# A memory-attention and feed-forward kernel: one quarter of the first 384 tokens in float16 halves, and a new order of all steps

## The chip, the cores and the metric

The kernel runs on one core of a Trainium2 chip. The metric is the time of one execution in microseconds (us); the table below gives the median of three runs. A profiled execution has a time of its own and a span, from its first instruction to its last. The engines are TensorE (PE, matrix products; its weight loads are shown as PEld), VectorE (DVE), ScalarE (ACT) and GpSimd (POOL); SyncE (SP) issues the transfers (DMA). Products are written to PSUM; all other tiles lie in SBUF.

## What is computed

The input has 8 batches of 8 heads, 576 positions and a head size of 64, with 32 memory slots per head. The feed-forward network has 512 inputs and 2048 hidden units.

```python
def _attn_ref(q, k, v, phi):
    a = softmax(phi)                        # over the 32 slots
    k_m = einsum('bhsm,bhsd->bhmd', a, k)
    v_m = einsum('bhsm,bhsd->bhmd', a, v)
    attn = softmax(q @ k_m.T / sqrt(64))    # over the 32 slots
    return attn @ v_m

def _moe_ref(x, w_in, w_out):
    h = x @ w_in
    g = maximum(0.01 * h, h)
    return g @ w_out
...
x = attn_out.transpose(0, 2, 1, 3).reshape(4608, 512)
return _moe_ref(x, w_in, w_out)
```

`softmax` is shorthand for the reference's maximum, exponential, sum and quotient. Both weight matrices come as 64-bit floats, 8 MB each.

## The kernel before

The kernel never forms the attention's output. For each batch it multiplies the memory values by `w_in` beforehand ("fold"), so that the first product of the network takes the attention weights `a` (8 heads by 32 slots, 256 rows) instead of the 512 features. The 2048 hidden units are cut into four quarters of 512, and these into 16 blocks of 128.

Tokens go through the network in groups. Groups 0, 1 and 2 are 384 tokens each, from batches 0 and 1; the later groups take 256 tokens, from batches 2 to 7. For each group and each pair of blocks ("unit" u, 8 of them) there is an up step (`up_products`, into `ph`), an activation (`leaky`) and a down step (`down_products`, three tiles of 128 tokens by 512 outputs, summed over all units in three PSUM tiles `po`).

Group 0 is done in float32: two matmuls of 128x384 per up step, with the folded weights in `w32`, and three of 128x512 per down step, against the float32 matrix in `wo`. All other groups are done in float16 halves: each operand is a high and a low part, and three products (high by high, low by high, high by low) stand for one, so 6 matmuls per up step and 9 per down step. A scalar factor per quarter scales the parts.

The weights are read as 64-bit words and made into float32 by integer and activation steps (`load`, `low`, `high`, `put`), their squares are summed for a bound (`squares`, lines 409 to 411), and later they are split into halves (`hi_part`, `lo_part`).

Every step has a name, and two long strings, `OPENING` and `LATER`, give the order in which the steps are issued; each engine runs its own instructions in that order. The names that matter below:

- `a0.phi`, `a0.k`, `a0.v`, `a0.q`: loads of batch 0. `A1`: the maximum of phi on VectorE (line 592), `A2`, `A3`, `B0`: the maximum spread over partitions (TensorE, lines 633 and 649, with VectorE between), `B1`, `B2`: subtraction and exponential (lines 658 and 664), `B3`: sums (lines 680 to 683), `C1`: products with k and v (line 698; `C10` is k, `C11` is v in batch 0), `C2`: the transposed sums (line 712), `C3`: scaled copies, `D1`: transposes (lines 777 and 785), `D3`, `D5`: copies (`D5` makes `vT`, line 805), `Q`: transposes of q (line 845), `E1`: scores (line 887; `E10` is its first half), `E2`: transposes of the scores (line 908), `S`: softmax of the scores, whose sixth step writes the weights `a`.
- `i0.ld1`, `i0.h1`, `i0.y1`, `i0.t1`, `i0.b`: load, low, high, put of piece 1, and squares, of quarter 0 of `w_in`; `o` stands for `w_out`. A piece is 768 or 512 columns. The loads go through eight buffers in turn.
- `f00.1`, `f00.2`: the fold of quarter 0 for batch 0 (line 1020) and its two copies to `w32` (line 1378). `W03.p`, `W03.h0`, `W03.l0`: the fold of batch 0, quarter 3 into halves.
- `u6.P0`, `u6.V0`, `u6.O0`: up step, activation and down step of group 0 (lines 1114, 1121, 1191); `P8`, `V8`, `C8`, `L8`, `O8` the same for groups 1 and 2, with the split into halves on VectorE (`C`, `L`). `p`, `v`, `s`, `c`, `l`, `d`, `x`, `z`: the later groups. `Z`: a tile's copy out and store.
- `z.4`: four float32 matmuls of ones, 128x512, that compute nothing ("idle products", line 1395). There are nine of them in four steps.
- `end0`, `end1`: the two halves of the last tile's output, copied by ScalarE and VectorE (lines 1176 and 1178), each with two stores issued by ScalarE and two by SyncE.

Of the kernel before, what the change touches and what calls it, by code (L numbers as in the profile page):

```python
# [22 lines left out]
A_SCALE = 2.0**13  # L23
# [27 lines left out]
i2.b u4.V0 a1.B20 u5.P0 a1.B3 o0.b a1.C10 i3.ld2 a1.Q0 i3.ld1 a1.C2 u5.V0 o1.b u2.O1 i3.y0 u5.P1
u4.V1 a1.C30 a1.C31 a1.C3k a1.C4 a1.D10 a1.D2 o2.b i3.h0 a1.D3 a1.Q1 i3.y2 i3.h2 a1.D11 a1.D4 u3.O1
i3.t2 a1.E1 o3.ld0 a1.D5 i3.y1 u4.O0 i3.h1 i3.t0 o3.h0 u5.V1 o3.y0 o3.ld2 u5.O0 a1.E20 i3.t1 a1.E21
i3.b ci.1 o3.ld1 a1.E22 f03.1 a1.S01 a1.S11 a1.S02 a1.S03 a1.S04 u4.O1 o3.y2 o3.y1 o3.h2 ci.2 o3.t0
f03.2 a1.S12 ci.3 ci.4 e. o3.h1 o3.t1 a1.S05 u6.P0 u6.V0 a1.S13 a1.S06 a1.S07 u6.P1 u7.P0 a1.S14
a1.S15 o3.t2 w0.2 u7.V0 u6.O0 a1.S16 o3.b w1.1 co.1 co.2 u7.O0 w1.2 co.3 u6.V1 co.4 u5.O1 o0.k0
a1.S08 o0.k1 o0.k2 u7.P1 e2. o0.l0 u7.V1 o0.l1 u6.O1 a1.S17 a1.S18 o0.l2 u7.O1
# [10 lines left out]
W01.h1 a2.phi a2.kv2 a2.kv1 o0.s0 W01.h0 a2.A1 Z0.0 o0.s1 a2.kv0 W01.l0 o0.m0 W01.l1 o0.m1 o0.n0  # L68
o0.n1 Z0.1 o0.s2 i0.k1 Z0.2 P8.0 P8.1 W11.p V8.0 a2.kv3 P9.0 o0.s3 V8.1 W11.h1 C8 P9.1 L8 W11.h0
a2.A2 W11.l1 V9.0 o1.k0 a2.A4 W11.l0 V9.1 O8.0 W02.h0 o1.l0 W02.h1 C9 o1.k1 O8.1 W02.l1 o1.k2 W02.l0  # L70
o0.m2 L9 o0.m3 W12.p o1.l2 o1.l1 P10.0 W12.h0 o0.n2 P10.1 V10.0 i0.k0 W12.l0 W12.h1 P11.0 o1.s0
V10.1 i0.k2 W12.l1 O9.0 V11.0 C10 o1.m0 o0.n3 L10 P11.1 o1.s1 O9.1 W03.h1 o1.n0 W03.h0 o3.s3 V11.1
P12.0 o1.m1 O10.0 C11 V12.0 o1.n1 L11 P12.1 o1.s2 O10.1 o1.m2 W03.l1 o1.s3 V12.1 W03.l0 a2.A3 o1.n2
o2.k0 C12 W13.p o2.k2 o2.l0 W13.h1 P13.0 W13.h0 W13.l1 P13.1 W13.l0 V13.0 o2.k1 L12 V13.1 O11.0
# [1419 lines left out]
```

## Time and profile before

| | |
|---|---|
| median of three runs | 648.58 us (647.6 to 649.02) |
| the profiled execution's own time | 647.19 us |
| its span | 645.3 us |
| TensorE busy | 632.7 us |
| VectorE, ScalarE, GpSimd busy | 515.0, 391.2, 29.5 us |
| moved by DMA | 61.16 MB |

The profiled execution took 647.19 us, 1.9 us more than its span; the runs that were timed are others. In the lines below, a row of the timeline gives start, duration, engine, source line, operation, output and inputs, sizes, the number of instructions merged into the row, and in brackets the idle time ahead of it with what ended it. The trace records a float32 matmul as two instructions. A row of the table by stretches gives the stretch and its length, busy time and instructions of PE, PEld, DVE, ACT and POOL, then TensorE's granted clock, the DMA engines' share, and GB/s.

### The profile page before, as it was taken

What the parts mean: (1) busy time and instruction counts of PE and PEld (TensorE: products, weight loads), DVE (VectorE), ACT (ScalarE), POOL (GpSimd) and SP (SyncE); (2) the same over time, 40 slices, a digit from 0 to 9 for tenths busy, and PEclk for the clock granted to TensorE, in tenths of its full rate; (3) what the DMA queues carried; (4) which work ended last, traced back from release to release, by engine and by line L of the source; (5) the groups of instructions that cost most, each with busy time, mean ns of one, the idle gap of its engine ahead of it and who ended that gap; (6) DMA issues with size and microseconds to landing.
All of it is one profiled execution on the core that took longest, in us unless ns stands there. A gap on an engine that the chain in (4) does not pass through costs nothing.

```text
span 645.3 us, 17189 instructions
## 1 busy us (share of the span) xinstructions
PE 632.7 (98%) x7304; PEld 480.4 (74%) x7304; DVE 515.0 (80%) x863; ACT 391.2 (61%) x671; POOL 29.5 (5%) x37
## 2 busy tenths in 40 slices
PE   6799999999999999999999999999999999999997
PEld 3445445665545788888888888897888888889896
DVE  5875889998997899899969975789977897575641
ACT  2898868765563556467556665655675476564543
POOL 0010111000001001002000010000010001000000
PEclk9999999999999999999999999999999999999999
DMA  9999813005601644431253011064104110010102
GB/s 263 405 389 290 279 44 118 15 13 99 196 3 31 139 156 66 124 105 42 33 138 124 6 30 42 22 125 149 34 20 85 18 30 23 13 28 8 34 1 51
DMA packets 85501, 61.16 MB, mean 95 GB/s; under 512 B 62000, under 2 KB 68656, under 8 KB 85424
## 3 DMA queue, kind: packets, MB, share of 16 engines
q1 hardware_dynamic: 85232, 59.94, 33.2%
q8 instruction: 57, 0.93, 0.6%
q14 instruction: 20, 0.16, 0.1%
q10 hardware_dynamic: 192, 0.13, 0.1%
HBM read 50.59 MB, written 9.45 MB: 93 GB/s over the span
## 4 chain that ended last, share of the span: by engine, by line
PE 94%; DMA 3%; ACT 1%; DVE 1%; issue 0%; SPq 0%; ACTq 0%
PE po L1302 31%; PE ph L1234 22%; PE po L1191 16%; PE ph L1114 8%; PE ph L1302 5%; PE pa L1020 4%; PE pa L698 3%; DMA arena<-in_moe_w_in_dram 2%; PE po L1339 2%; PE pa L861 1%; DMA wo<-in_k_dram 1%; DMA arena<-in_q_dram 0%; ACT arena L397 0%; ACT wi L411 0%; PE pa L887 0%
## 5 line engine op out<-in xcount | busy, mean ns | idle before, releaser
L1302 PEld LDWEIGHTS <-arena 128*128 128x128 f16 x2184 | 209.8, 98 | 31.9 <-issue 8.6
L1250 ACT ACTIVATE wi<-ph,g_sc 128x256 f32<-128x256 f32 (+1 forms) x224 | 98.6, 465 | 160.9 <-PE ph L1234 155.8
L1234 PE MATMUL ph<-a,w_mem 128*128 128x256 f16 (+3 forms) x1440 | 144.8, 246 | 0.1
L1234 PEld LDWEIGHTS <-w_mem 128*128 128x128 f16 x1440 | 114.5, 98 | 13.8 <-issue 3.0
L1302 PE MATMUL po<-wo,arena 128*128 128x256 f16 x936 | 122.1, 273 | 0.0
L1302 PE MATMUL po<-arena 128*128 128x256 f16 x936 | 122.0, 273 | 0.0
L1191 PE MATMUL po<-wo,arena 128*128 128x512 f16 (+1 forms) x384 | 110.3, 433 | 0.0
L1279 DVE TENSOR_TENSOR arena<-arena 128x1024 f16<-128x1024 f32 x52 | 63.5, 1221 | 21.9 <-ACT arena L1275 21.9
L1279 DVE TENSOR_TENSOR arena<-wi,arena 128x768 f16<-128x768 f32 (+1 forms) x60 | 54.7, 911 | 9.5 <-ACT arena L1275 9.5
L1271 DVE TENSOR_TENSOR arena<-wi 128x256 f32<-128x256 f32 x104 | 40.4, 430 | 25.4 <-ACT wi L1250 24.8
L1275 ACT CAST arena<-arena 128x1024 f16<-128x1024 f32 x52 | 54.4, 1046 | 7.9 <-DVE arena L1271 7.6
L1114 PE MATMUL ph<-a,w_mem 128*128 128x192 f16 (+2 forms) x304 | 52.2, 317 | 0.0
L1191 PEld LDWEIGHTS <-arena 128*128 128x128 f16 x288 | 27.9, 98 | 29.6 <-issue 0.6
L1275 ACT CAST arena<-wi 128x768 f16<-128x768 f32 (+1 forms) x60 | 46.6, 776 | 1.5
L1271 DVE TENSOR_TENSOR arena<-wi,arena 128x256 f32<-128x256 f32 x104 | 45.7, 439 | 1.8
L1302 PE MATMUL ph<-wo,arena 128*128 128x256 f16 x312 | 42.6, 273 | 0.0
L985 POOL TENSOR_TENSOR a<-t,a 128x1024 f16<-128x1024 f32 (+2 forms) x16 | 21.9, 1384 | 428.1 <-ACT a L980 428.1
L1191 PEld LDWEIGHTS po<-wo,arena 128*128 128x128 f32 x96 | 17.7, 190 | 20.3 <-issue 18.2
L1020 PE MATMUL pa<-wi,vT 64*32 64x512 f16 (+1 forms) x704 | 28.9, 420 | 1.2 <-ACT vT L805 1.2
L1114 PEld LDWEIGHTS <-w_mem 128*128 128x128 f16 x240 | 20.7, 98 | 10.3 <-issue 4.1
L1121 ACT ACTIVATE arena<-ph,g_sc 128x384 f32<-128x384 f32 x32 | 18.4, 581 | 15.7 <-PE ph L1114 15.4
L1053 ACT ACTIVATE w_mem<-pa 128x512 f16<-128x512 f32 x40 | 22.7, 596 | 7.5 <-PE pa L1020 6.6
(216 smaller groups left out, 752.9 us busy)
## 6 DMA issues: line engine op xcount, KB each, us to landing
out_dram<-obs SPq DMA_DIRECT2D x140, 64.0 KB, 1.7
arena<-in_k_dram SPq DMA_DIRECT2D x28, 288.0 KB, 4.6
arena<-in_v_dram SPq DMA_DIRECT2D x28, 288.0 KB, 5.1
arena<-in_q_dram SPq DMA_DIRECT2D x96, 72.0 KB, 2.8
arena<-in_moe_w_in_dram SPq DMA_DIRECT2D x12, 512.0 KB, 9.6
arena<-in_moe_w_out_dram SPq DMA_DIRECT2D x8, 768.0 KB, 7.9
arena<-in_phi_dram SPq DMA_DIRECT2D x7, 576.0 KB, 5.6
arena<-in_q_dram SPq DMA_DIRECT2D x4, 576.0 KB, 8.7
```

Of the source, the lines that this page charges most:

```text
L698: nc.tensor.matmul(var["pk"][g][hh * M:(hh + 1) * M, cs], ld["phi"][rows, hh, j, :], ld["kv", hh][rows, kinds[0]:kinds[-1] + 1, j, :], sta ...
L985: nc.gpsimd.tensor_tensor(piece(lo, tb), piece(t2, tb), piece(hi, tb), ALU.subtract)
L1020: nc.tensor.matmul(pf[g][cols, :], lhs, rhs, start=(n == 0), stop=(n == len(passes) - 1), tile_position=(g * D, hh * M),)
L1053: nc.scalar.activation(tiles(halves(w16(b, j), g)[:, 0]), w(g), AF.Copy, scale=ws)
L1114: nc.tensor.matmul(ph[:, t0:t0 + n * SB], lhs, rhs, start=(m == 0), stop=(m == len(seq) - 1))
L1191: nc.tensor.matmul(po, lhs, rhs, start=(f == 0 and m == 0), stop=(f == NQ * NF - 1 and m == len(seq) - 1),)
L1234: nc.tensor.matmul(ph[:, t0:t0 + n], lhs, rhs, start=(m == 0), stop=(m == len(seq) - 1))
L1250: nc.scalar.activation(dst, ph, AF.Prelu, scale=g_sc2[:, j:j + 1], alpha=SLOPE)
L1271: nc.vector.tensor_tensor(gt[:, x], y, z, op)
L1275: nc.scalar.copy(dst[:, 0], src)
L1279: nc.vector.tensor_tensor(dst[:, 1], src, dst[:, 0], ALU.subtract)
L1302: nc.tensor.matmul(acc, g[:, x, s, u], rhs, start=(h == 0 and j == 0 and u == 0 and m == 0), stop=(j == NQ - 1 and u == 1 and m == 2), ski ...
```

## The change

Quarter 3 of group 0 (units 6 and 7) leaves the float32 path. Its up steps take halves of the folded weights and halves of `a`, which two new steps make (`A0.h`, `A0.l`); its activation goes through the split that groups 1 and 2 use (`u6.C`, `u6.L`). The sums over quarters 0 to 2 lie in three PSUM tiles under another scale, so they are copied aside first (`Y0`, ScalarE), their places are used anew for quarter 3, and at the end one VectorE instruction for each tile scales that result and adds what was set aside. The fold of quarter 3 for batch 0 goes straight from PSUM into halves; the step `f03` is gone. Groups 1 and 2 run through the quarters in the order 3, 2, 1, 0.

```diff
+    Q32 = NQ - 1
...
     wi_s, wo_s = (
-        [t.bitcast(F16).rearrange("p (i x) -> p i x", i=2) for t in ts[:NQ]] for ts in (wi, wo)
+        [t.bitcast(F16).rearrange("p (i x) -> p i x", i=2) for t in ts]
+        for ts in (wi[:NQ], wo[2:] + wo[:1])
...
+    def full(G, u):
+        return G == 0 and u < 2 * Q32
...
+    def quarter(G, u):
+        return u // 2 if G == 0 else NQ - 1 - u // 2
...
+    def a0_part(i):
+        src = a_f32(0)[:, 0:2].rearrange("p tb (g x) -> p tb g x", g=NG)
+        hi, lo = a0_halves[:, :, 0], a0_halves[:, :, 1]
+        if i == 0:
+            nc.scalar.copy(hi, src)
+        else:
+            nc.gpsimd.tensor_tensor(lo, src, hi, ALU.subtract)
...
-            if G == 0:
+            if full(G, u):
                 seq = [
-                    (w32[f // NF][g][:, fs], a_f32(b)[:, tb:tb + n, g * SB:(g + 1) * SB])
+                    (w32[j][g][:, fs], a_f32(b)[:, tb:tb + n, g * SB:(g + 1) * SB])
                     for g in range(NG)
                 ]
             else:
                 seq = [
-                    (halves(w16(b, f // NF), g)[:, x, fs], a[:, tb:tb + n, y, g, :])
+                    (halves(w16(b, j), g)[:, x, fs], a[:, tb:tb + n, y, g, :])
                     for g in range(NG) for x, y in ((0, 0), (1, 0), (0, 1))
                 ]
...
+    def set_aside(t):
+        nc.scalar.activation(obs[:, t * E:(t + 1) * E], pos["32"][t], AF.Copy, scale=1.0 / WT)
...
     def store(G, t, po):
         ob = obs[:, t * E:(t + 1) * E]
-        nc.scalar.activation(ob, po, AF.Copy, scale=row_scale(G, t))
+        if G == 0:
+            nc.vector.scalar_tensor_tensor(ob, po, row_scale(G, t), ob, ALU.mult, ALU.add)
+        else:
+            nc.scalar.activation(ob, po, AF.Copy, scale=row_scale(G, t))
         send(G, t, ob)
...
-        if G == 0:
+        if full(G, u):
             seq = [(g[:, i, cs], wo[j + 1][:, es])]
         else:
             seq = [(g[:, x, i, cs], wo_s[j][:, y, es]) for x, y in ((0, 0), (0, 1), (1, 0))]
...
-a0.phi0 a0.A10 z.4 a0.phi1 a0.A11 a0.A2 a0.k a0.A3 a0.B0 a0.q0 a0.B10 a0.B11 a0.B20 a0.q1 a0.B21
+a0.phi0 a0.phi1 a0.A11 a0.A10 a0.A2 a0.A3 a0.B0 a0.B10 a0.B20 a0.k a0.B11 a0.B21 a0.C10 a0.B3 a0.C2
...
-z15.0 d53.2 p55.3 v55.3 c55.1 z15.1 d53.3 l55.1 d54.0 d54.1 d54.2 d54.3 d55.0 d55.1 end0 d55.2 d55.3
-end1
+d53.3 d54.0 d54.1 d54.2 d54.3 d55.2 d55.0 d55.3 d55.1 end1 end0
```

The buffers of the split halves move with the order of the quarters (the halves of `w_out` into `wo2`, `wo3`, `wo4`, `wo0`; the sums of pairs of blocks that the later groups use start in `wo1`). Both strings of steps are new throughout. Three places of the new order follow.

TensorE at the very start of the program, before (L1395 are the idle products, L633 and L649 are A2 and B0, L698 is C10):

```order
L1489 UNCONDITIONAL_BRANCH
L1395 MATMUL pa<-ones 128x512 x4
L633 MATMUL pa<-ident,r1k 128x128
L649 MATMUL pa<-r1k,ones 64x128 x2
L698 MATMUL po<-wo_92,wi_88 32x64 x2
```

and in the changed program, whose lines for the same steps are 635, 651 and 700:

```order
L1520 UNCONDITIONAL_BRANCH
L635 MATMUL pa<-ident,r1k 128x128
L651 MATMUL pa<-r1k,ones 64x128 x2
L700 MATMUL po<-wo_92,wi_88 32x64 x2
L700 MATMUL po<-wo_93,wi_88 32x64 x2
```

The four idle products at the head are gone from there; A2 is TensorE's first work.

TensorE from C2 (L712) over D10 (L777) and the two halves of the scores (L887) to the products with v (L698), before:

```order
L712 MATMUL po<-ident,r1k 128x128
L1395 MATMUL pa<-ones 128x512
L777 MATMUL pa<-ident,x_k 96x128 x4
L887 MATMUL pa<-wi_87,kT 32x192 x24
L887 MATMUL pa<-wo_91,kT 32x192 x24
L1395 MATMUL pa<-ones 128x512 x3
L698 MATMUL po<-wo_92,wi_88 32x64 x2
```

and in the changed program:

```order
L714 MATMUL po<-ident,r1k 128x128
L1431 MATMUL pa<-ones 128x512 x3
L779 MATMUL pa<-ident,x_k 96x128 x4
L1431 MATMUL pa<-ones 128x512
L889 MATMUL pa<-wi_87,kT 32x192 x24
L889 MATMUL pa<-wo_91,kT 32x192 x24
L1431 MATMUL pa<-ones 128x512 x4
L700 MATMUL po<-wo_92,wi_88 32x64 x2
```

Three idle products stand ahead of D10 where one stood, one more ahead of the scores, and four behind them where three stood.

ScalarE at the end of the program, before (L1250 are activations, L1275 casts, L1326 scales a finished tile, L1176 is the copy of `end0`, L1165 issues stores):

```order
L1275 CAST arena<-wi_89 128x256
L1326 ACTIVATE obs<-obs,osc 128x512
L1176 ACTIVATE obs<-po,osc 128x256
L1165 DMA out_dram<-obs 32x256 x4
L1489 UNCONDITIONAL_BRANCH
```

and in the changed program:

```order
L1303 CAST arena<-wi_89 128x256
L1184 DMA out_dram<-obs 32x256 x2
L1201 ACTIVATE obs<-po,osc 128x256
L1184 DMA out_dram<-obs 32x256 x2
L1520 UNCONDITIONAL_BRANCH
```

The two stores of `end1`'s half now stand ahead of the copy of `end0`'s; on TensorE the last down steps are d55.2, d55.0, d55.3, d55.1 in place of d55.0 to d55.3.

More of the change, by code (lines that the diff above doesn't have):

```diff
@@ L51 @@
[L51 to L56, printed above, removed]
@@ L67 @@
 LATER = """
[L68 to L72, printed above, removed]
@@ L1049, in w @@
         def w(g):
-            return tiles(w32[j][g]) if b == 0 else by_tile(src["w"][g])
+            return tiles(w32[j][g]) if b == 0 and j < Q32 else by_tile(src["w"][g])
         def hi_part(g):
@@ L1119, in leaky @@
     def leaky(dst, ph, G, u):
-        sc = H_SCALE0 if G == 0 else g_sc[:, u // 2:u // 2 + 1]
+        sc = H_SCALE0 if full(G, u) else g_sc[:, quarter(G, u):quarter(G, u) + 1]
         nc.scalar.activation(dst, ph, AF.Prelu, scale=sc, alpha=SLOPE)
@@ L1189, in down_products @@
             seq = [(g[:, x, i, cs], wo_s[j][:, y, es]) for x, y in ((0, 0), (0, 1), (1, 0))]
+        u0, u1 = (0, 2 * Q32) if full(G, u) else (2 * Q32 if G == 0 else 0, NU)
         for m, (lhs, rhs) in enumerate(seq):
             nc.tensor.matmul(
-                po, lhs, rhs, start=(f == 0 and m == 0),
-                stop=(f == NQ * NF - 1 and m == len(seq) - 1),
+                pos["32" if full(G, u) else G][t], lhs, rhs, start=(f == 2 * u0 and m == 0),
+                stop=(f == 2 * u1 - 1 and m == len(seq) - 1),
             )
     def down(G, u, i):
-        if (u, i) == (0, 0):
-            pos[G] = [ps_o.tile([P, E], F32, name="po") for t in range(NT)]
+        if i == 0 and u in (0, 2 * Q32 if G == 0 else 0):
+            pos["32" if full(G, u) else G] = [
+                ps_o.tile([P, E], F32, name="po") for t in range(NT)
+            ]
         for t in range(NT):
@@ L1372 @@
         opening(u)
-    for j in range(NQ):
+    for i, key in enumerate("hl"):
+        steps[f"A0.{key}"] = lambda i=i: a0_part(i)
+    for t in range(NT):
+        steps[f"Y0.{t}"] = lambda t=t: set_aside(t)
+    for j in range(Q32):
         def products(j=j):
@@ L1381 @@
         bounds(kind, steps)
-    steps["e."] = fold_scales
+    for b in range(FB):
+        steps[f"e{b}."] = lambda b=b: fold_scales(b)
     for b in range(B):
@@ L1400 @@
         steps[f"z.{n}"] = lambda n=n: idle_products(n)
-    def all_bounds():
-        even_out()
-        for b in range(FB):
-            out_scale(b)
-    steps["e2."] = all_bounds
+    steps["e2."] = even_out
     def unit(m):
```

291 lines of the change are left out of this document (153 added, 138 removed).

## The prediction

> **What bounds the kernel now.** I read the page's shares first, then a table of busy time by stretch, then the list of what TensorE waited for.
>
> ```profile
> span 645.3 us, 17189 instructions
> ...
> PE 632.7 (98%) x7304; PEld 480.4 (74%) x7304; DVE 515.0 (80%) x863; ACT 391.2 (61%) x671; POOL 29.5 (5%) x37
> ...
> 20.00:30.00 10.00, 7.82 (x171) 3.75 (x172) 9.11 (x18) 8.35 (x14) 0.87 (x2) 1.00 1.03 410
> 30.00:640.00 610.00, 609.90 (x6862) 468.86 (x6861) 493.56 (x826) 375.86 (x649) 27.77 (x28) 1.00 0.31 84
> ...
> PE po L698 <- ACT wi L664: 1.7, 1, 1.7
> ```
>
> From 30 to 640 us TensorE is busy 609.90 of 610.00 us at a granted clock of 1.00, and the longest wait on the list, 1.7 us for the exponential of phi, belongs to the first 30 us, as all others do. So the time has three parts that add up: an **opening** until the first product of the feed-forward network, an unbroken **stream** of matmuls whose length is the sum of its instructions, and a **tail** of a few microseconds. An engine beside TensorE matters only where it makes the stream pause. The execution took 647.19 us, its span 645.3; the median of the three timed runs, 648.58, lies 1.39 above it. I work out a difference and add it to both.
>
> **The stream.** These pieces of the chain that ended last give the price of a matmul where matmuls of one kind follow each other.
>
> ```profile
> 31.10 2.58 PE ph L1114 x8
> 33.68 2.57 PE po L1191 x6
> ...
> 116.67 1.94 PE po L1191 x9
> ...
> 144.83 1.95 PE ph L1114 x12
> ```
>
> A float32 matmul is recorded as two. Up products in float32 (384 columns): 2.58 / 4 = 0.645 us each; down products in float32 (512 columns): 2.57 / 3 = 0.857; in float16, 1.95 / 12 = 0.1625 and 1.94 / 9 = 0.2156. The last quarter of group 0 is four blocks of 128 units. Each had 2 float32 up products and 3 float32 down products, and now has 6 and 9 in float16.
>
> - Up: 4 x (2 x 0.645 - 6 x 0.1625) = 4 x 0.315 = 1.26 us less.
> - Down: 4 x (3 x 0.857 - 9 x 0.2156) = 4 x 0.631 = 2.52 us less.
>
> The stream gets **3.8 us** shorter, all of it on the path. The fold of quarter 3 runs as the same 8 float32 matmuls as before, now as step W03.p. Reversing the quarters of groups 1 and 2, and moving the sums' buffers, changes operands and no count. What is added lies beside TensorE: three copies of 128x512 out of PSUM on ScalarE (Y0), two casts and two subtractions on VectorE, a cast of 128x768 on ScalarE and a subtraction on GpSimd (A0); two ScalarE copies of the old quarter go. Their cover is the 39% of the span in which ScalarE is idle, and u6.P0, W12.p, P9 and P8.0, which stand on TensorE between the last float32 product of the group and the first into the new accumulators. Without that cover three copies of about 0.6 us would cost 1.8.
>
> Whether the new order keeps the stream unbroken the trace cannot show. The tightest place that I find is batch 1's attention: before, two up steps and a down step stood on TensorE between B0 and C10; now only two up steps do (4 x 0.645 = 2.6 us), against a subtraction and an exponential in between.
>
> ```profile
> L658 DVE TENSOR_TENSOR arena<-arena,pa 128x1152 f32<-128x1152 f32 x1 | 1.4, 1354 | 0.9 <-PE pa L649 0.9
> L664 ACT ACTIVATE arena<-arena 128x1152 f32<-128x1152 f32 x7 | 8.1, 1157 | 0.4 <-DVE arena L658 0.4
> ```
>
> 1.35 + 1.16 plus two hand-overs is 2.6: no slack, and a pause of 0 to 0.5 us. I put pauses at 0.2 us, from 0 (as before) to 1.0 (two more such places).
>
> **The opening.** Here are TensorE's rows up to the first product, then the rows of VectorE and ScalarE that it waits for.
>
> ```profile
> 0.99 6.34 PE L1395 MATMUL pa<-ones 128*128 128x512 f32 x8 [0.99 <-POOL ones L269]
> 7.17 0.27 PE L633 MATMUL pa<-ident,r1k 128*128 128x128 f32 x1
> ...
> 10.54 0.37 PE L698 MATMUL po<-wo,wi 64*32 64x64 f32 x10 [1.68 <-ACT wi L664]
> ...
> 11.97 0.23 PE L698 MATMUL po<-wi,wi 64*32 64x64 f32 x2
> 12.89 0.33 PE L712 MATMUL po<-ident,r1k 128*128 128x128 f32 x1 [0.69 <-DVE r1k L683]
> 13.06 1.02 PE L1395 MATMUL pa<-ones 128*128 128x512 f32 x2
> 14.73 0.73 PE L777 MATMUL pa<-ident,x_k 128*96 128x128 f32 x4 [0.65 <-ACT x_k L743]
> 16.13 1.15 PE L887 MATMUL pa<-wi,kT 32*32 32x192 f32 x48 [0.67 <-ACT kT L799]
> ...
> 18.22 1.07 PE L887 MATMUL pa<-wo,kT 32*32 32x192 f32 x39 [0.15 <-issue]
> 19.95 2.84 PE L1395 MATMUL pa<-ones 128*128 128x512 f32 x6 [0.66 <-DVE t L908]
> ...
> 23.32 0.25 PE L698 MATMUL po<-wi,wi 64*32 64x64 f32 x2 [0.27 <-DMA wi<-in_v_dram]
> ...
> 25.01 0.23 PE L698 MATMUL po<-wi,wi 64*32 64x64 f32 x2
> ...
> 27.34 1.09 PE L1020 MATMUL pa<-wi,vT 64*32 64x512 f32 x16 [1.16 <-ACT vT L805]
> ...
> 29.35 1.53 PE L1114 MATMUL ph<-a,w_mem 128*128 128x384 f32 x4
> ```
>
> ```profile
> 3.75 2.18 DVE L592 TENSOR_REDUCE r1k<-wi 128x64 f32<-128x576 f32 x2 [3.75 <-DMA wi<-in_phi_dram]
> ...
> 19.31 1.05 DVE L908 STREAM_TRANSPOSE t<-pa 128x384 f32<-128x384 f32 x2 [0.49 <-PE pa L887]
> 20.39 0.95 DVE L928 TENSOR_REDUCE tm<-t 128x24 f32<-128x768 f32 x1
> 21.89 0.69 DVE L406 SCALAR_TENSOR_TENSOR wi<-arena 128x512 uint32<-128x512 uint32 x1 [0.55 <-ACT arena L386]
> 22.50 0.95 DVE L931 TENSOR_TENSOR t<-t,tm 128x768 f32<-128x768 f32 x1
> 23.37 0.95 DVE L406 SCALAR_TENSOR_TENSOR wi<-arena 128x768 uint32<-128x768 uint32 x1
> ...
> 4.57 1.28 ACT L664 ACT_TABLE_LOAD   x1 [4.57 <-DMA wi<-in_phi_dram]
> ...
> 24.36 1.91 ACT L411 ACTIVATE wi<-wi 128x2048 bf16<-128x2048 f32 x1
> ...
> 27.03 0.25 ACT L805 COPY vT<-pa 128x128 f32<-128x128 f32 x1
> 27.18 0.95 ACT L386 ACTIVATE arena<-arena 128x768 uint32<-128x768 uint16 x1
> ...
> 28.58 1.07 ACT L1378 COPY w_mem<-pa 128x512 f32<-128x512 f32 x2
> ```
>
> The first eight idle records take 6.34 us, 0.79 each; the six at 19.95 take 2.84, 0.47 each. So TensorE starts at about half rate and is at full rate once these have run. The new order drops them.
>
> 1. The first maximum now starts with the half of phi that lands last, at 4.5 us by the table load's wait: 4.5 + 2.18 = 6.7, and L633's step starts then, not at 7.17.
> 2. C10 then begins near 10.3. It took 1.66 us (10.54 to 12.20); at half rate up to 3.3. C2, which waits for VectorE's sums (to 12.89 in its row, some 0.2 earlier now), starts between 12.7 and 13.6: 13.1.
> 3. z.3 stands where z.1 stood. Six records take 2.6 (0.857 / 2 = 0.43 each, as in the stream) to 5.1 (twice that); I take 3.5, because some of C10 has already run. D10 starts at 13.1 + 0.3 + 3.5 = 16.9, not 14.73.
> 4. From D10 to the end of E1 it was 4.56 us (14.73 to 19.29). z.1 (1.02) now stands between D10 and E10, and D10's 0.73 plus 1.02 passes the 1.40 after which E10 started; less the waits that go, 4.7. E1 ends at 21.6, 2.3 later.
> 5. VectorE flips (1.05), takes the maximum (0.95) and subtracts (0.95), then puts two pieces of the weights (0.6 and 0.9); ScalarE squares them (1.95 with its read-out), decodes one piece (0.85) and copies vT (0.25). That is 7.5 us, to 29.1 with little between; the old path took 8.05 to its fold at 27.34. Fold 1.09 and the first copy 0.55: the first product at **30.7**, not 29.35.
>
> Steps 3 to 5 have a second branch: v is now queued on SP behind another 512 KB piece, 1.3 us at the 410 GB/s of the row from 20 to 30 us, which moves its landing from 23.3 to 24.6. Were all else early, C11 (1.9), z.1, the x_v transpose (0.3) and vT would put the product at 29.7. The opening is therefore later by 0.3 to 3.1 us (z.3 wholly at half rate, D10 at 18.7); I take **1.3**.
>
> [...]
>
> **The tail.** Before, both halves of the last tile were copied by different engines, the last by VectorE as soon as its products were done.
>
> ```profile
> 635.43 6.06 PE L1339 MATMUL po<-wo,arena 128*128 128x256 f16 x54
> ...
> 640.21 0.47 ACT L1176 ACTIVATE obs<-po,osc 128x256 f32<-128x256 f32 x1 [3.04 <-PE po L1339]
> 640.72 2.17 ACTq L1165 DMA_DIRECT2D out_dram<-obs  x4
> 641.52 0.48 DVE L1178 TENSOR_SCALAR obs<-po,osc 128x256 f32<-128x256 f32 x1 [4.63 <-PE po L1339]
> ```
>
> Now VectorE's half is done first and ScalarE's last, and two DMA issues stand before that copy in ScalarE's queue, waiting for VectorE. d55.1, the last step, is six matmuls of 6.06 / 54 = 0.112, 0.67 us. VectorE ends 0.48 after d55.3, some 0.15 before the stream's end. Four issues spread over 2.17 us with a wait for VectorE among them, 0.4 each; two of them hold ScalarE's copy until 0.65 after the stream's end, where VectorE's started 0.03 after it. Tail: **0.6 us** later (0 if an issue does not hold the engine, 0.8 at most).
>
> **Sum.** -3.8 + 0.2 + 1.3 + 0.6 = -1.7 us: 645.5 beside the execution's 647.19, and **646.9** beside the median.
>
> **The rivals.**
> - *The opening is not later.* C10 and z.3 run at full rate and z.3 hides behind the transfers; only the 0.3 of v's branch remains: -3.8 + 0.2 + 0.3 + 0.5 = -2.8, 645.8; without the tail's cost 645.2. For it: before, the weights' landing at 19 us and ScalarE's squares, not attention alone, held the fold. Against it: z.3 stands on the scores' own path. Chance 0.17.
> - *Half rate through z.3*: C10's small products count for little and z.3 runs at 0.85 a record, so D10 starts at 18.7 and the opening is 2.9 later: -3.8 + 0.3 + 2.9 + 0.6 = 0, 648.6. For it: the eight records at the start spent about five microseconds at half rate. Against it: C10 keeps TensorE busy for 1.7 to 3.3 us ahead of z.3. Chance 0.18. [...]
> - *Slower: half rate until the scores are done.* If z.3 too fails to raise the clock, D10, z.1, E10 and E1 (0.73 + 1.0 + 1.15 + 1.6) double, 4.5 us on top of the 2.9: 648.6 + 4.5 = 653.1. It decides the sign from the point where the opening is 4.5 us late (3.8 + 1.3 less 0.6). Against it: z.3 is sustained work of 3 to 5 us. Chance 0.05. A stream with over 2.5 us of pauses would end on that side too; 0.04.
> - *The halves save nothing*, because 36 + 24 weight loads replace 20: then +2.1. Against it: the float16 pieces above run at 0.2156 and 0.1625 with their loads hidden. Chance 0.02.
>
> **How the numbers follow.** The forecast (opening 0.6 to 2.3 later) has 0.54. About 0.2% or 1.3 us is what a measurement of this kernel can tell from no change, and the forecast itself reaches from -2.7 (opening 0.6 later, no pause) to -0.5 (2.3 later, pauses of 0.4); 0.7 of it is faster by more than that. Faster: 0.54 x 0.7 + 0.17 = 0.55. Slower: 0.05 + 0.04 + 0.02 = 0.11, less what of it stays within 1.3: 0.09. Same: 0.36. The range runs from the first rival without the tail's cost, 645.2, less 0.2, to the second, 648.6, plus 0.3 (the three runs of before spread over 1.42): 645.0 to 648.9.
>
> **What would show it.** Right: idle records at 0.85 each at the start of z.3; D10 near 17 us; first up product near 30.7; no wait of TensorE over 0.3 us after it; from there to the last matmul 3.6 us less than the 612.1 of before; last ScalarE copy starting 0.6 us behind the last matmul. Wrong: a first product before 29.8 or after 32.5, a wait of a microsecond or more inside the stream, or float16 products of quarter 3 dearer than 0.22 and 0.17 us.

## The result, and the profile after

The changed kernel is slower: 665.46 us median of six runs (662.39 to 667.31) against 648.80 us of six runs of before (646.99 to 649.57), a ratio of 1.0257 with an interval of 1.0224 to 1.029. The forecast was 646.9 us, in a range from 645.0 to 648.9, with a chance of 0.09 for slower.

The profiled execution took 666.92 us, 1.5 above the median, its span 665.0; the mean granted clock of the six executions was 0.992 to 0.997, so not all of them lost the same. First the lines of its page that answer to those shown of before, then the same stretches of the table of busy time (columns: length, then busy us and count of TensorE, its weight loads, VectorE, ScalarE and GpSimd, granted clock, DMA share, GB/s), with two stretches of ten microseconds more.

```profile
span 665.0 us, 17217 instructions
...
PE 634.2 (95%) x7324; PEld 480.9 (72%) x7324; DVE 525.0 (79%) x870; ACT 384.4 (58%) x670; POOL 34.0 (5%) x38
```

```profile
20.00:30.00 10.00, 8.62 (x202) 4.52 (x202) 7.76 (x14) 6.94 (x9) 0.00 (x0) 0.83 1.03 404
30.00:640.00 610.00, 594.41 (x6704) 451.79 (x6703) 502.06 (x830) 364.91 (x634) 33.08 (x30) 0.99 0.31 84
222.00:232.00 10.00, 7.01 (x87) 5.31 (x85) 9.41 (x14) 3.57 (x7) 0.00 (x0) 0.83 0.37 88
492.00:502.00 10.00, 7.20 (x177) 5.97 (x175) 9.20 (x11) 4.15 (x7) 2.72 (x3) 0.83 0.01 2
```

The row from 30 to 640 us is the whole story in short. Before, TensorE was busy 609.90 of these 610.00 us at a clock of 1.00. Now it is busy 594.41 at 0.99: the stream has holes. The last two rows show what two of the holes look like. TensorE has 7 us of work in 10 while VectorE works 9.4 and 9.2, and the clock of 0.83 says that for some 3.4 of the 10 us the clock stood at half.

The list of what TensorE waited for (total, times, longest) has new entries at its head. The first entry's 6.7 is the wait for phi at the very start; its other wait, 1.5, and all of the next three lie in the stream, where before had none.

```profile
PE pa L635 <- DVE r1k L594: 8.2, 2, 6.7
PE pa L863 <- DVE arena L838: 3.7, 3, 3.0
PE ph L1262 <- ACT wi L1278: 3.3, 3, 2.8
PE po L1330 <- DVE arena L1307: 2.6, 2, 1.7
```

Where the 19.7 us between the two spans (645.3 and 665.0) lie, added up from TensorE's rows:

| part | forecast | profiled execution |
|---|---|---|
| opening: first product at 32.85 instead of 29.35 | +1.3 | +3.5 |
| the last quarter in halves, from start of step to start of next | -3.8 | -3.5 (up 5.26 to 4.17, down 10.49 to 8.07) |
| pauses of TensorE in the stream above 0.12 us, 18 of them | +0.2 | +14.4 |
| two stretches of 3.41 us at half clock in the stream, half of each | none | +3.4 |
| tail: last matmul to the end of the span, 4.46 instead of 3.77 | +0.6 | +0.69 |
| rest, not traced to places | none | +1.3 |

So the halves brought what was worked out for them, the tail cost what was worked out for it, and the stream that was taken as unbroken lost 18 us.

**Two pauses read closely.** The longest pause is at 226.53. TensorE's rows (start, length, line), then SyncE's queue of DMA issues, then VectorE's rows:

```profile
222.72 0.82 PE L1262 MATMUL ph<-a,w_mem 128*128 128x256 f16 x6
226.53 1.24 PE L863 MATMUL pa<-arena,x_k 64*32 64x64 f32 x48 [2.99 <-DVE arena L838]
```

```profile
205.24 11.65 SPq L577 DMA_DIRECT2D arena<-in_q_dram  x16
217.01 0.56 SPq L540 DMA_DIRECT2D arena<-in_phi_dram  x1
```

```profile
217.84 0.29 DVE L341 TENSOR_SCALAR mdiag<-ident,m 128x128 f32<-128x128 f32 x1
221.68 2.16 DVE L594 TENSOR_REDUCE r1k<-arena 128x128 f32<-128x1152 f32 x1 [3.55 <-DMA arena<-in_phi_dram]
223.75 2.63 DVE L838 STREAM_TRANSPOSE arena<-arena 128x1152 f32<-128x1152 f32 x2
```

The scores of batch 3 (L863) wait for the two flips of its q (L838). Those flips stand in VectorE's order behind the reduction of batch 4's phi (step a4.A1, L594), and that reduction stands still for 3.55 us, because its load is issued at 217.01, behind sixteen issues for q that hold SyncE for 11.65 us. The scores need nothing of batch 4. In before, the same load was issued at 210.64, between the two halves of q, and VectorE's reduction did not wait for it:

```profile
210.64 0.56 SPq L538 DMA_DIRECT2D arena<-in_phi_dram  x1
```

```profile
217.28 2.14 DVE L592 TENSOR_REDUCE r1k<-arena 128x128 f32<-128x1152 f32 x1
```

The second is at 497.73. VectorE, ScalarE, GpSimd, TensorE:

```profile
493.47 2.70 DVE L1299 TENSOR_TENSOR arena<-wi,arena 128x256 f32<-128x256 f32 x2
...
496.26 1.04 ACT L1303 CAST arena<-arena 128x1024 f16<-128x1024 f32 x1 [2.37 <-DVE arena L1299]
497.21 0.47 ACT L1278 ACTIVATE wi<-ph,g_sc 128x256 f32<-128x256 f32 x1
...
493.77 2.69 POOL L987 TENSOR_TENSOR a<-t,a 128x1024 f16<-128x1024 f32 x2 [95.24 <-ACT a L982]
...
497.73 1.44 PE L1262 MATMUL ph<-a,w_mem 128*128 128x256 f16 x6 [2.80 <-ACT wi L1278]
```

Two additions (L1299) that take 0.88 us elsewhere take 2.70: the second is held until GpSimd's first subtraction (493.77 to 495.89) is done. A cast on ScalarE waits for it, the leaky step (L1278) stands behind the cast, and TensorE waits for the leaky step. The six up products then take 1.44 us instead of 0.82: the clock has just been halved. Before has such a hold too, with no pause of TensorE behind it:

```profile
245.34 2.70 DVE L1271 TENSOR_TENSOR arena<-wi,arena 128x256 f32<-128x256 f32 x2
```

### The profile page after: what moved, and what is told of

It reads as the page before. It is cut to its first block, busy times and chain, and to the rows that moved or that the text cites. A ratio compares the mean times of both kernels' runs of the same rounds, so it can differ in the third digit from the quotient of the medians.

```text
span 665.0 us, 17217 instructions
## 1 busy us (share of the span) xinstructions
PE 634.2 (95%) x7324; PEld 480.9 (72%) x7324; DVE 525.0 (79%) x870; ACT 384.4 (58%) x670; POOL 34.0 (5%) x38
## 5 line engine op out<-in xcount | busy, mean ns | idle before, releaser
L1330 PEld LDWEIGHTS <-arena 128*128 128x128 f16 x2184 | 210.5, 98 | 35.5 <-issue 5.7
L1278 ACT ACTIVATE wi<-ph,g_sc 128x256 f32<-128x256 f32 (+1 forms) x224 | 95.4, 464 | 137.8 <-PE ph L1262 121.4
L1262 PEld LDWEIGHTS <-w_mem 128*128 128x128 f16 x1440 | 114.7, 98 | 18.6 <-issue 7.9
L1217 PE MATMUL po<-wo,arena 128*128 128x512 f16 (+1 forms) x396 | 105.9, 419 | 0.0
L1307 DVE TENSOR_TENSOR arena<-wi,arena 128x768 f16<-128x768 f32 (+1 forms) x60 | 54.9, 920 | 13.1 <-ACT arena L1303 10.8
L1217 PEld LDWEIGHTS <-arena 128*128 128x128 f16 x324 | 31.3, 98 | 36.7 <-issue 1.9
L1299 DVE TENSOR_TENSOR arena<-wi,arena 128x256 f32<-128x256 f32 x104 | 45.7, 439 | 1.8
L1135 PE MATMUL ph<-a,w_mem 128*128 128x192 f16 (+2 forms) x288 | 45.3, 307 | 1.1 <-ACT w_mem L1417 0.7
L1299 DVE TENSOR_TENSOR arena<-wi 128x256 f32<-128x256 f32 x104 | 41.4, 439 | 1.7
L1142 ACT ACTIVATE arena<-ph,g_sc 128x384 f32<-128x384 f32 x36 | 20.1, 577 | 21.2 <-DVE arena L1156 14.6
L1061 DVE SCALAR_TENSOR_TENSOR w_mem<-pa,w_mem 128x512 f16<-128x512 f32 x40 | 26.9, 679 | 6.5 <-ACT w_mem L1055 6.4
L1135 PEld LDWEIGHTS <-w_mem 128*128 128x128 f16 x264 | 23.2, 98 | 10.1 <-issue 3.2
```

The costliest lines, as they stand in the source:

```text
L1061: nc.vector.scalar_tensor_tensor(tiles(t[:, 1]), w(g), ws, tiles(t[:, 0]), ALU.mult, ALU.subtract)
L1135: nc.tensor.matmul(ph[:, t0:t0 + n * SB], lhs, rhs, start=(m == 0), stop=(m == len(seq) - 1))
L1217: nc.tensor.matmul(pos["32" if full(G, u) else G][t], lhs, rhs, start=(f == 2 * u0 and m == 0), stop=(f == 2 * u1 - 1 and m == len(seq) - 1),)
L1262: nc.tensor.matmul(ph[:, t0:t0 + n], lhs, rhs, start=(m == 0), stop=(m == len(seq) - 1))
L1278: nc.scalar.activation(dst, ph, AF.Prelu, scale=g_sc2[:, j:j + 1], alpha=SLOPE)
L1299: nc.vector.tensor_tensor(gt[:, x], y, z, op)
```

## The experiments

Theory A at the outset: single places in the new order. VectorE, ScalarE and SyncE run their steps in the written order, so one step that waits for a transfer (3.55 us above) or is held beside GpSimd (2.70 instead of 0.88) delays what stands behind it, and the two pauses above cost the clock too (0.83 in both rows). Rival B: VectorE is too full in this order, so that a pause taken away comes back at the next place.

**Four waits for transfers put later.**

```
- c2.0 d0.0 a4.A1 a3.D3 a3.Q1 a3.Q0 ... p4.0 a3.E23 a3.S01
+ c2.0 d0.0 a3.D3 a3.Q1 a3.Q0 ... p4.0 a3.E23 a4.A1 a3.S01
  (and a5.Q0 behind s14, a6.Q0 behind l27.0, a7.Q0 behind s34)
```

> After, with four VectorE steps that stand still for a transfer put later in VectorE's order and nothing else changed: the reduction of batch 4's phi behind the flips and scores' steps of batch 3 (it stood ahead of them at 221.68 and waited 3.55 us), and one flip of q each of batches 5, 6 and 7 behind VectorE's next work for the stream (they waited 3.38, 3.17 and 2.62 us). Theory A (VectorE works in order, so a step that waits for a transfer holds up the stream's steps behind it): the pauses of TensorE at 226.53 (2.99), 443.75 (1.70), 446.68 (0.29) and 515.63 (0.87) go, and with the first of them the stretch at half the clock from 227.72 to 231.13 (1.7 us lost): 7.5 us less than the 666.9 of after's profiled execution, some 659.4. Rival B (VectorE has too much to do in this order, and a pause that is taken away comes back at the next place): pauses of the same sum return within some 20 us behind these places, and the time is within 2 us of 666.9.

660.91 us (657.98 to 663.35, ratio 1.0198, 1.0158 to 1.0238), 4.6 below after. The pause at 226.53 is gone; TensorE's rows there now run on:

```profile
220.67 0.82 PE L1262 MATMUL ph<-a,w_mem 128*128 128x256 f16 x6
221.41 1.23 PE L863 MATMUL pa<-arena,x_k 64*32 64x64 f32 x48
```

The half clock behind it and the pauses at 443.75 and 515.63 are gone as well. But where after paused for 0.96 at 263.84, this kernel pauses for 1.02 at 254.35 and 1.49 at 259.73. A likely reason, not shown, is that the pause taken away had let VectorE catch up. All pauses of the stream together fell from 14.4 to 10.9, not by the 5.9 expected. A is right on the places, and B is right in part.

**GpSimd's subtraction moved at two places.**

```
- nc.gpsimd.tensor_tensor(
+ (nc.vector if b == 3 else nc.gpsimd).tensor_tensor(
      piece(lo, tb), piece(t2, tb), piece(hi, tb), ALU.subtract
  (a3.S08 one step later, behind l5.1; a6.S07 behind v34.1)
```

> After, with the subtraction that GpSimd makes for the lower half of the attention's output changed at two places: batch 3's runs on VectorE, one step later; batch 6's stays on GpSimd, and the ScalarE copy that it waits for stands three stream steps later, so that it starts elsewhere. Theory A (while GpSimd subtracts, one VectorE instruction is held until it is done, 1.6 to 1.9 us, and at these two places that is work for the stream): VectorE's rows of 1.78 us at 260.97 and of 2.24 us at 493.93 go back to 0.17 and 0.42, TensorE's pauses at 263.84 (0.96) and 265.27 (0.30) and at 497.73 (2.80) go, and with the last one the half clock from 497.37 to 500.79 (1.7): 5.8 us less than 666.9, some 661. For batch 6 a VectorE instruction elsewhere is then held just as long. Rival B (the stretch is short of VectorE's time and the hold is only what shows it): the pauses shrink by less than 1 us together.

662.65 us (659.54 to 665.66, ratio 1.0221, 1.0178 to 1.0264), 2.8 below after, which the scatter of the two kernels' runs does not tell from no gain; the evidence is in the rows. VectorE's rows of after and then of this kernel, at the same instructions:

```profile
260.97 1.78 DVE L726 TENSOR_SCALAR r<-r 128x2 f32<-128x2 f32 x1
```

```profile
259.53 0.17 DVE L726 TENSOR_SCALAR r<-r 128x2 f32<-128x2 f32 x1
...
263.22 1.42 DVE L987 TENSOR_TENSOR a<-t,a 128x1024 f16<-128x1024 f32 x2
```

An operation on two numbers per partition took 1.78 us and takes 0.17. The whole subtraction on VectorE costs 1.42, less than the 1.6 for which GpSimd's held it. The pauses of 0.96 and 0.30 are gone. At the second place the additions take 0.88 again and the pause fell from 2.80 to 0.98 without a fall of the clock. The moved subtraction (498.49 to 500.64) held no instruction of VectorE, though one was expected to be held just as long: beside it ran a reduction of 2.27 (2.19 in the median of its kind) and an addition of 0.43 that reads PSUM, as elsewhere. At these two places A is confirmed and B's bound (under 1 us together) passed. But longer pauses elsewhere (1.46 at 338.8, 1.41 at 462.2) gave most of it back: all pauses of the stream together are 13.9, against 14.4 in after.

**Idle products at the head.** z.4 put behind a0.phi1, and z.3 behind a0.C2 taken away.

> After, with idle products at the head of TensorE's order as in before (eight of 128x512, before the first reduction's transposes) and without the six behind the projections' first scores. Theory A (the opening is late because TensorE's clock is at half until 16.09 and again from 22.92 to 26.33): the granted clock is full from some 6.5 us, the memory's products start ahead of 17.19, and the first product of the stream comes at 29.4 to 31.2 instead of 32.85: 1.7 to 3.5 us less than 666.9. Rival B (the q that lands after 20 us, or the weights' copies ahead of the first product, set it): the first product comes within 0.5 us of 32.85 and the time within 0.5 us.

665.69 us (665.37 to 666.38): no gain in time, as B had it, but neither side had the first product. The clock was full from 5.42 to 15.66, then fell for 13.65 us, and the first product came at 34.97. What the run showed together with the two before it is that the opening's time is not fixed by its order alone. These are the same four idle products, eight records (step z.4 behind the flip of the scores), of after, of the first and of the second experiment, whose openings are identical to the letter:

```profile
22.52 5.40 PE L1431 MATMUL pa<-ones 128*128 128x512 f32 x8 [0.64 <-DVE t L910]
```

```profile
20.76 3.70 PE L1431 MATMUL pa<-ones 128*128 128x512 f32 x8 [0.51 <-DVE t L910]
```

```profile
22.84 5.85 PE L1431 MATMUL pa<-ones 128*128 128x512 f32 x8 [0.65 <-DVE t L910]
```

3.70 at full clock (1.00 from 20 to 30 us), 5.40 and 5.85 where the clock fell back to half in the opening (0.83 and 0.66 there); the first product came at 30.12 in the second of these, at 32.85 and 33.62 in the others. The forecast of 30.7 was near the opening that keeps its clock.

**All edits together.** The three kernels' edits, a1.A2 behind u2.P1, and before's last steps (`d55.0 d55.1 end0 d55.2 d55.3 end1`).

> After, with the edits of the three kernels beside it together, and two more: the transposes of batch 1's reduction on TensorE stand behind the next twelve products of the stream (pause of 1.50 at 56.62), and the last four steps are in before's order (the last half of the result stored behind two blocks instead of four). Theory A (the changed kernel lost what it lost to single places of its order, and the halves save what was worked out for them): 7.5, 5.8, 1.7 to 3.5, 1.5 and 0.65 off 666.9, some 648 to 650, no pauses above 0.5 us in the stream. Rival B (VectorE's load is what binds): the pauses come back elsewhere, and the time stays above 655.

654.67 us (653.5 to 658.62, ratio 1.0109, 1.0074 to 1.0144): 10.8 us below after, where some 17 were expected. 9.0 us of pauses stay, the longest at places that had none or a shorter one in after (1.96 at 458.3, 1.18 at 338.2, 1.03 at 256.7). Time to ask whether the late order as a whole is too tight.

**The late order of before.** The orders of after and of before agree on the set of steps done by the 589th, but for ten. So this kernel runs after's order to there (191 us) and before's from there, with the halves.

```
  ... V22.1 V21.1 C21 a2.S08 O19.1        (after's order, 589 steps)
+ then every step not yet done, in the order in which before names it
```

> After, with its own order of steps as far as the 589th step (some 191 us of its profiled execution, where the first unit of the late part begins) and from there every remaining step in the order that before gives it; the float16 halves stay. Theory A (the order searched anew leaves too little room between VectorE, ScalarE and TensorE, and the halves are what they were said to be): TensorE's pauses behind 191 us go (11.2 us of them, 216.87 to 515.63) with the two stretches at half the clock (3.4), and the end is before's (0.65): about 15 us less than after in the same state of the opening, 650 to 652. Rival B (the halves, with the work they add to VectorE and ScalarE, leave no order of this kind free of pauses): pauses of over 5 us stay in the late part and the time stays above 657.

651.62 us (650.09 to 657.54; ratio 1.0052, 1.0026 to 1.0078): 13.8 below after, as A had it. Table of busy time, the row that answers to the one above:

```profile
30.00:640.00 610.00, 605.38 (x6857) 465.23 (x6858) 500.29 (x837) 376.50 (x649) 31.77 (x30) 1.00 0.31 83
```

VectorE is busy for 500.29 of these 610 us, and for 502.06 in after. So what costs in the late part is not the amount of its work, as B had it, but the order.

How long ahead of TensorE's start was each result ready that it waits for on another engine, from 35 us on? Less than 0.3 us ahead were 42 of 482 waits in before, 103 of 447 in after, and here 34 of 120 up to 200 us (after's order) and 26 of 363 behind (before's order). By this count close calls are more than twice as frequent in the new order; a held instruction or a late transfer then lands on TensorE. The count goes with the pauses and does not prove their cause.

**Before's first 31 steps as well.**

> The kernel beside it, and the first 31 steps in before's order too (loads of phi, k and q, idle products at the head of TensorE's order, up to the scores of the second half of the heads). Theory A (the opening is late because of the order of its first steps, and with them of the clock): the first product of the stream comes at 29.4 to 31 instead of 30.1 to 33.6, and the time is 1 to 3 us below the kernel beside it, 647.5 to 650; with the halves' 3.5 us saved it can come level with before. Rival C (what stands behind the 31 steps sets the first product: the copies for the weights and softmax): first product within 0.5 us of the kernel beside it.

657.0 us (654.94 to 658.4, five runs): 5.4 above the kernel without them. With the head's idle products the clock was full from 6.12, but fell at 23.19, and the first product came at 32.63, where it came at 29.98 in the kernel without them. Neither forecast came true: the opening got later, by a fall of the clock behind the moved steps.

**The reverse: before with two of these moves.** Idle products from the head to behind a0.C2, and a4.phi issued behind a3.q1.

```
- a0.phi0 a0.A10 z.4 a0.phi1 ... a0.B3 a0.C2 i0.ld2
+ a0.phi0 a0.A10 a0.phi1 ... a0.B3 a0.C2 z.4 i0.ld2
- W23.l0 a4.phi a3.C2 p0.3 a3.C30 a3.q1 O22.1
+ W23.l0 a3.C2 p0.3 a3.C30 a3.q1 a4.phi O22.1
```

> Before, with two of the suspected moves put in: the idle products at the head of TensorE's order stand behind the projections instead, and the load of batch 4's phi is issued behind the second half of batch 3's q instead of ahead of it. Theory A (these two kinds of move are what costs): the first product comes 1.7 to 4 us later than 29.35, at a clock of half in part of the opening; the reduction of phi that VectorE began at 217.28 waits until some 221, and TensorE pauses 2.5 to 4 us between 222 and 230, with 1.7 us more where the clock falls: 4 to 9 us slower than before in all. Rival B (before's order has enough room to take them in): under 1.5 us slower, no pause above 0.5 us.

654.28 us (652.82 to 656.78; ratio 1.0096, 1.0068 to 1.0123), 5.5 slower than before, from one load issued behind another and four idle products moved. VectorE, then TensorE:

```profile
222.64 2.15 DVE L592 TENSOR_REDUCE r1k<-arena 128x128 f32<-128x1152 f32 x1 [4.09 <-DMA arena<-in_phi_dram]
...
228.41 2.19 PE L861 MATMUL pa<-arena,x_k 64*32 64x64 f32 x36 [2.72 <-DVE arena L836]
```

A pause of 2.72, half clock from 228.32 to 231.74 (1.7), and a first product 0.96 later: 5.4 together, beside the 5.6 by which this execution (652.82) lies above the profiled one of before (647.19). For the late load the mechanism is shown in both directions. The opening's part was smaller than A had it (1.7 to 4 us).

**The waits filled.** Three idle products directly ahead of a3.E1 and of p34.3, in after. Nothing else moves.

> After, with three idle products of 128x512 (2.6 us at full clock) put into TensorE's order directly ahead of the two longest waits of its stream: the scores of batch 3 that wait until 226.53 (2.99 us idle) and the up products that wait until 497.73 (2.80). VectorE's and ScalarE's orders stay, so the waits end when they did. Theory A (the clock falls for 3.41 us where TensorE is idle for about half of such a stretch or more; in the traces so far 1.70 us and more in one stretch brought it down and 1.64 did not): with the waits filled the stretches at half clock behind 227 and 497 do not come, the pauses shown shrink to some 0.4 us, and the kernel is 2 to 3.4 us faster than after. Rival B (the clock falls for another cause at these places, or the waits end later because the fillers hold a buffer): half clock stays, or the time does not fall.

662.99 us (660.03 to 668.91; ratio 1.0221, 1.0182 to 1.026), 2.5 below after, again within the scatter of the two. TensorE's rows at the first place:

```profile
220.73 2.74 PE L1431 MATMUL pa<-ones 128*128 128x512 f32 x6
223.40 1.33 PE L863 MATMUL pa<-arena,x_k 64*32 64x64 f32 x48
```

VectorE's steps are as late as they were, yet neither stretch at half clock comes (one comes at 441.04 instead, behind a pause of 1.70 that after has too). So at these two places the clock fell because TensorE was idle: with the waits filled it is 1.00 from 216 to 226 and from 488 to 498 us, and the six up products at the second place take 0.81 us instead of 1.44. With one stretch at half clock instead of two, first to last product take 626.4 us instead of 627.7, 1.3 less, near the 1.7 that half of a stretch of 3.41 us comes to. The bounds named beforehand, 1.70 and 1.64, are not those that the stretches of the stream give; the last section has the count.

**The groups of small matmuls.** The kernel with before's late order still paused inside two groups, a4.C10 and a7.C10, with no releaser:

```profile
244.06 2.26 PE L700 MATMUL pa<-arena 64*32 64x128 f32 x137
247.76 0.42 PE L700 MATMUL pa<-arena 64*32 64x128 f32 x7 [1.43 <-issue]
```

First they were cut in two, with a step of the stream between the halves (`slots_of((0, 1), range(5))`, then `range(5, KJ)`).

> The kernel with the late order of before, and in it the products that sum batch 4's and batch 7's keys and values by phi (144 small matmuls of some 15 ns each) cut in two after five of nine rows of blocks, with one step of the stream between the halves. Theory A (the pauses of 1.43 at 247.76 and 1.29 at 491.84 inside these groups, for which no row shows a releaser, are TensorE's supply of instructions, which 288 instructions in 2 us outrun, and six or twelve products of 110 ns give it the time back): both pauses go or fall under 0.5 us, 2 us or more off the 651.6, some 649. Rival B (the last rows wait for a transfer or for ScalarE's exponentials): the pauses stay, now in the second half. Rival C (the supply stops at a certain place in the program, whatever runs there): pauses of the same length a few steps further on.

651.34 us (650.27 to 656.5, 12 runs; before 649.11; ratio 1.0041, 1.0023 to 1.0059). The stops, from one weight load to the next, fell from 1.80 and 1.64 us to 0.71 and 0.43, but at the very same place of TensorE's program: they shrank, as A had it, and kept their place, as C had it. That the supply of instructions is the cause is the author's reading; the place of the stops is what is shown. The divided groups still take 3.4 and 3.3 us, and the median gained only 0.3.

Then the cut and fuller idle products, four at the head and four behind a0.C2 (eight records each):

> The same, with eight idle products at the head of TensorE's order and eight instead of six behind the projections. Theory A (the first product's time hangs on the granted clock, and the clock on how much of each stretch of 3.41 us TensorE is busy: with these fillers no stretch of the opening is idle for half of it): full clock from some 6 us to the end in the profiled execution, first product at 29 to 30, and single times within 1.5 us of each other, where the kernel with the late order had 650.1 to 657.5; median 0 to 1.5 us below the kernel beside it, some 648. Rival B (a stretch between 19 and 23 us still falls short, as in the two kernels with a head tried so far): half clock from some 19 to 23 us on, first product at 31 or later, 1 to 3 us slower than the kernel beside it.

650.40 us (648.34 to 654.66; ratio 1.0022, 1.0003 to 1.0042), the lowest of the medians. The clock was full from 6.85, at half once more from 10.26 to 13.67, and full from there; the first product came at 30.82. Executions whose mean clock was 1.0 and those at 0.995 to 0.997 still lie some 2.5 us apart (649.1 and 651.7 in the mean), so neither A nor B holds cleanly.

Then three early waits, in after's part of the order:

> The kernel with the late order of before, the divided groups and the warm head, with three steps moved in its first 100 us: GpSimd's subtraction for batch 0's halves (at 44.90 in that kernel's profiled execution, with VectorE's next row only at 46.99) goes behind the fifth unit's leaky step, some 80 us; a leaky step of unit 2 goes ahead of a conversion on ScalarE (u4's product waited 0.4 for it until 57.28); the last quarter of batch 1's k and v is issued before another conversion's steps (0.55 waited until 60.09). Theory A (what the halves save is given back by single waits of 0.4 to 1.1 us in the first third): the pauses at 53.65 and 60.09 go, 1 to 1.6 us below the kernel beside which it stands, median some 649.0, level with before. Rival B (a wait removed there comes back within 20 us, since VectorE and ScalarE are full until 100 us): under 0.4 us gained.

650.72 us (649.47 to 654.14; before 649.03; ratio 1.0025, 1.0009 to 1.0041). The pauses at 53.65 and 60.09 are gone and the profiled execution's stream is 0.3 us shorter; the median says B.

Last, the groups whole again, but 24 and 18 weight loads earlier in TensorE's program. In this kernel the exponentials of batch 4's phi stand ahead of the subtraction of the maximum, so its numbers for that batch are others; the work and its length are the same.

> The kernel with the late order of before, its groups of small matmuls whole, the three early steps moved as in the kernel with the early edits, no warm head and six idle products less than there were in after's opening (three and three of them left, in two places). The groups of batch 4 and batch 7 stand 24 and 18 weight loads earlier in TensorE's program than in the kernel where they paused for 1.43 and 1.29 us (three and two steps of the stream ahead, with the steps before them on VectorE and ScalarE moved along), so that they end ahead of the place in the program at which the supply stopped there. Theory A (the supply of instructions stops at a fixed place, and products of 110 ns behind the group cover it as they do in before): both groups take 2.2 to 2.7 us instead of 4.05 and 4.11, 3 us less, median 648 to 649.5, at or a little below before's. Rival B (the supply runs dry behind any such group; the pause moves behind it, onto the stream): pauses of over 0.7 us within 2 us behind the groups, median above 650.5.

650.97 us (649.18 to 653.63; before 649.08; ratio 1.0023, 1.0002 to 1.0044).

```profile
243.74 2.90 PE L700 MATMUL pa<-arena 64*32 64x128 f32 x144
```

Both groups run through, 2.84 and 2.94 us to the start of the next step instead of 4.05 and 4.11, and no pause follows within 2 us but one of 0.22, as A had it for the groups. The time did not follow: with fewer idle products the clock fell at 30.84, on the first products of the stream.

## Why the prediction was wrong, point by point

- **The stream's gain was right.** 3.8 us forecast, 3.5 measured (1.09 of 1.26 for the up products, 2.42 of 2.52 for the down products). That the halves save nothing is excluded. Before's late order, with the halves in it, shows that they were not what cost the 13.8 us that this order took away.
- **The step that failed** is the sentence "Whether the new order keeps the stream unbroken the trace cannot show", with the 0.2 us (0 to 1.0) put beside it. The pauses were 14.4 us. The one tight place that I named, between B0 and C10 of batch 1, has no pause above 0.12; the pause near it, 1.49 at 56.62, comes from the reduction ahead of it. Three mechanisms stood in that term's place. Transfers waited for in VectorE's order: shown by the four moves, and in reverse in before. GpSimd's subtraction holding VectorE: shown by taking it off GpSimd (1.78 us to 0.17). And generally too little room: 23% of the waits ended within 0.3 us of TensorE's start, against 9%; putting the old late order back removed the late pauses but for those inside the two groups of small matmuls and one of 0.29. The trace of before could have given the first of them: q's 16 issues at some 0.7 us each, a load moved behind them, some 4.6 us to land, and a reduction of 2.1 us with the flips behind it.
- **A term was missing:** behind the pauses of 2.99 and 2.80 the clock was at half for 3.41 us each, from 227.72 and from 497.37. Half of both, 3.4 us, was lost. The forecast had used the clock for the opening alone, though it priced a stream with pauses as a rival (0.04).
- **The opening was mis-sized**, 3.5 instead of 1.3. The steps were right as far as they went: C10 at 10.3 (measured 10.52), D10 at 16.9 (17.19). Where the clock then holds, the same opening gives its first product at 30.1, 0.6 earlier than forecast; in the profiled execution it fell again at 22.92. I took the clock as once up, always up. No run shows the reach of 0.6 to 2.3 that the forecast gives the opening: in the changed kernel and those built on it the first product came from 0.6 us later than before's (29.98, with the late order of before) to 5.6 (34.97, with idle products at the head). Of the rivals, "half rate through z.3" comes near the size (2.9) and misses the place: D10 came at 17.19 and not at 18.7, and it is mainly z.4, behind the scores, that ran slow.
- **The tail was right**: 0.6 forecast, 0.69 measured. ScalarE's last copy started 0.81 behind the last matmul, behind its two issues, where 0.65 was forecast.
- **Two of the signs named for being wrong came**: a first product after 32.5, and waits of a microsecond and more inside the stream. In the forecast's own reach, -2.7 should read -2.6 (-3.8 + 0.6 + 0.6); nothing hangs on it.
- **No version beat before.** The best medians, 650.4 to 651.0, are 0.2 to 0.25% above it. With the old late order and the halves, the stream still is 1.6 to 3.0 us longer than before's and the opening 0.6 to 3.3 later. By step, the 3.5 us of the halves are given back mainly in the first 200 us, in waits that the new order has there, and in the two groups of small matmuls. That an order could be found that keeps the 3.5 us is likely but was not shown.

## What to carry to other kernels

Where an order of steps is written out or searched for, look first at what each in-order engine stands behind: for every step that waits for a transfer, find the issue, count what is queued ahead of it, and ask who waits for the steps behind. A stream without pauses is worth its slack: judge an order by how early results are ready, not only by whether the sum of the work fits. And price a pause of TensorE at up to 1.7 us on top where it leaves 1.91 us or more of a stretch of 3.41 idle, as in the nine cases counted below; idle products that filled it took that part away at both places tried.

## What the runs showed of the hardware

- **In the stream, the clock fell behind a stretch that was a little over half idle.** Over thirteen traces (all but that of the last experiment) I cut the stream into stretches of 3.41 us, on whose edges the clock changes (in after the changes at 26.33 and 227.72 lie 59 of them apart, those at 231.13 and 497.37 lie 78 apart), and added up TensorE's idle time in each. All nine stretches with 1.91 us or more of idle time (1.91 to 2.81) were followed by 3.41 us at half clock; none with 1.57 or less was. A pause of 1.70 did it or not according to how the stretches cut it: in after, at 443.75, it did not. In the opening the same count does not part the cases: 1.55 in after (ahead of the fall at 22.92) and 1.75 in the last experiment (ahead of 30.84) brought the clock down, and 1.75 in the kernels with idle products at the head and with all edits did not. What exactly is counted stays open.
- **Inside groups of small matmuls, TensorE stopped at places that lie multiples of 256 of its instructions apart.** Counting weight loads, matmuls and semaphore instructions from the program's start, every stop of over 0.35 us without a releaser inside a group of small matmuls, in before too (0.41 at 24.42), lies at 194 modulo 256: numbers 706, 2754, 5058 and 11458. The page's DMA queue for instructions moves 0.93 MB in 57 packets, 16 KB each; before's page has 14608 weight loads and matmuls, 256 to a packet. That a stop is a wait for such a packet is the author's estimate from these numbers and was not shown. The two groups of 288 instructions at some 7.6 ns each that had two such places inside ran the 256 between them in 1.9 us and stood at the second, up to 1.8 us; moved by 48 and 36 instructions, so that only one lies inside, they did not stand.
- **Beside GpSimd's subtraction, some VectorE instructions stood until it was done.** While GpSimd subtracted 128x1024 (2.1 to 2.4 us), one VectorE instruction stood until it was done, 1.6 and 1.8 us longer than elsewhere at the two places tried, be it an addition or an operation on two columns. Both have all their inputs in SBUF. Instructions that read PSUM were not held, in any of some 70 cases over all traces: in after, beside the subtraction from 328.10 to 330.23, an addition with one input in PSUM took 0.69 as elsewhere, and the next, with both in SBUF, 1.99 instead of 0.95. Before has such a hold too (2.25 us at 245.80 for an addition of 0.42) and no pause behind it.
